# One-bank accumulator tiles for the later steps, and another order of the early steps, in a chunked linear-attention kernel with token routing

## The chip, the cores and the metric

The program runs on one core of one Trainium2 chip. A core has a matrix engine (TensorE, PE in the rows, with its weight loads as PEld), two engines that work along partitions and can read the accumulator memory PSUM (VectorE, DVE, and ScalarE, ACT), GpSimd (POOL), which cannot, and SyncE (SP), which here only issues transfers. Each engine runs its own stream in order, and semaphores order the streams against each other. The metric is the device time of one execution in microseconds (us); lower is better.

## The reference

For 4 batches, 8 heads, 768 positions and head size 64, the first half is decayed linear attention in blocks of 64. `lam` is one decay per head:

```
intra = (q_b k_b^T * Dmask) v_b              # Dmask[i,j] = lam^(i-j), i >= j
inter = (q_b * lam^(pos+1)) kv_state
out_b = intra + inter
kv_state = lam^64 * kv_state + (k_b * lam^(63-pos))^T v_b
```

The heads are then joined to rows x of 512. The second half routes tokens: scores = x . w_gate for each of the 768 positions of a batch, the 128 positions with the highest scores are taken, and for these out = x + sigmoid(score) * (relu(x w1) w2), with w1 of 512x1024 and w2 of 1024x512. All other rows stay x.

## The kernel before

**Steps.** The work is cut into 24 steps g of 128 positions, 6 for each batch. Steps 0 to 9 are "wide" (`wide(g)`, line 66): the 128 positions are one block of the attention, with masks and powers made for 128 (lines 135 to 158). Steps 10 to 23 are "narrow": two blocks of 64. Meanwhile w1 and w2 are loaded, and in narrow steps the expert products of an earlier batch are put in as "pieces" (`expert`, `products`), three to a step.

**A step's parts.** `transposes` makes q^T and k^T in PSUM with TensorE, `moved` copies them to SBUF with ScalarE (qT, kT). `queries_decayed` (POOL) makes qs from qT, `keys_decayed` (POOL) kd. `scores` multiplies kT and qT into the PSUM tile `su`; `masked` (DVE) takes it times the mask to p. `state_products` multiplies kd and v into `uu` (wide) or `su` (narrow), and `next_state` (DVE) adds the decayed old state. `from_scores` and `from_states` add up the output in the tile `o`; `outputs` (ScalarE) copies it out, `store` sends it to memory, `gate_scores` (DVE) takes the routing score. For the ranking, `row` transposes a column of scores, `compare` (DVE) makes a table of who beats whom, `column_sums` adds its columns up, and at the end of a batch `find`, `take` and `fetch` turn ranks into a list of tokens and gather their rows.

**PSUM.** It has 8 banks of 512 floats per partition. Four tiles of two banks each fill it: `su`, `o`, `uu`, `tt` (lines 181 to 184). In wide steps `tt` holds the transposes: q^T and k^T use the same columns, one after the other. In narrow steps the four banks of `uu` and `tt` are dealt out in turn by `bank()` (line 188) to transposes, rows, column sums and pieces, as slices of the two tiles:

```
free = [tt[:, 0], tt[:, 1]]
...
free[:0] = [uu[:, 0], uu[:, 1]]
```

**What sets the order.** The program order is written out by hand (`wide_step`, and the loop at the end). Each engine's stream follows it. The semaphores are put in by the framework: an instruction waits for those before it, on other engines, that touch the same tile.

Of the kernel before, what the change touches and what calls it, by code (L numbers as in the profile page):

```python
# [17 lines left out]
def kernel(  # L18
# [146 lines left out]
    def narrow_constants(g):  # L165
        if g == 0:
            for c in range(2):
                nc.scalar.copy(out=ident_c[half[c]], in_=ident[half[c], half[c]])
        elif g <= NHP:
            hp = g - 1  # L170
            for hh in range(2):
                h = 2 * hp + hh
                nc.vector.tensor_tensor_scan(
                    out=mask[:, hh, hp, :], data0=lam_b[:, h : h + 1].broadcast_to([128, C]),
                    data1=ident_c[:], initial=0.0, op0=ALU.mult, op1=ALU.add,
                )
        elif g == NHP + 1:
            nc.scalar.copy(out=kpow[:].rearrange("p a b -> p b a"), in_=mask[:, :, :, C - 1])
            nc.scalar.copy(out=decay[:], in_=qpow[:, :, C - 1 : C].broadcast_to([128, NHP, D]))
# [40 lines left out]
    pending = {}  # L220

    def transposes(g, name):
        if g >= NG:
            return
        t = loaded[g][1 if name == "qT" else 0]
        if not wide(g):
            tp = bank()
            pending[g, name] = tp[:]
            for hp in range(NHP):
                nc.tensor.transpose(  # L230
                    tp[:, hp * L : (hp + 1) * L], in_=t[:, 2 * hp : 2 * hp + 2, :],
                    identity=ident[:],
                )
            return
        tp = tt[:, :, : 2 * L]
        pending[g, name] = tp
        if name == "qT":
            to = tp.rearrange("p u (a i r) -> p u a r i", a=2, r=2)
        else:
            to = tp.rearrange("p u (a r i) -> p u a r i", a=2, r=2)  # L240
        for a in range(2):
            for r in range(2):
                for u, w in FOUR:
                    nc.tensor.matmul(  # L244
                        to[half[w], u, a, r], lhsT=t[half[u], 4 * a + 2 * w + r, :],
                        rhs=ident[half[u], half[u]], start=True, stop=True,
                        skip_group_check=True,
                    )

    def moved(g, name):  # L250
        if g >= NG:
            return
        dst = att.tile([128, NHP, L], FP32, name=name)
        src = pending.pop((g, name))
        if wide(g):
            nc.scalar.copy(out=dst[:].rearrange("p (u a) i -> p u (a i)", u=2), in_=src)  # L256
        else:
            nc.scalar.copy(out=dst[:].rearrange("p a i -> p (a i)"), in_=src)  # L258
        (qTs if name == "qT" else kTs)[g] = dst
# [15 lines left out]
    def scores(g, part=(0, 1)):  # L275
        if g >= NG:
            return
        if wide(g):
            qT, kT = qTs[g], kTs[g]
            if 1 in part:  # L280
                del qTs[g], kTs[g]
            for a in part:
# [10 lines left out]
        qT, kT = qTs.pop(g), kTs.pop(g)  # L293
# [140 lines left out]
    def settle(g):  # L434
        seen = mod.tile([128, 2], FP32, name="seen")
        if g % NT:
# [42 lines left out]
    def row(g):  # L479
# [8 lines left out]
        pb = uu[:, 0, 2 * D : 2 * D + L] if wide(g + 1) else bank()[:, :L]  # L488
# [3 lines left out]
        nc.scalar.copy(out=rows_[b][:, t * L : (t + 1) * L], in_=pb)  # L492
        fresh[g] = pb

# [25 lines left out]
    def column_sums(g):  # L520
# [4 lines left out]
        col = uu[:, 1, 2 * D : 2 * D + t] if wide(g + 2) else bank()[:, :t]  # L525
# [25 lines left out]
    def tokens(b, i):  # L551
        e = hits_.pop((b, i))
        pk = uu[:, 1, 3 * D : 3 * D + 2] if len(free) == 2 else bank()[:, :2]
# [171 lines left out]
    def wide_step(g):  # L725
        n = g + 1
        if g >= 0:
            if NGR:
                row(g - 1)
                column_sums(g - 2)  # L730
                compare(g - 1)
            queries_decayed(n)
# [7 lines left out]
        keys_decayed(n + 1)  # L740
        if wide(n):
            scores(n, (0,))
            from_states_wide(n, 1)
            scores(n, (1,))
        else:
# [9 lines left out]
        if NGR:  # L755
            if ends(g - 3):
                take((g - 3) // NT)
            if ends(g - 2):
                find((g - 2) // NT)

    for g in range(-1, NG):
# [3 lines left out]
        if g < 0:  # L765
            transposes(0, "qT")
            moved(0, "qT")
            transposes(0, "kT")
            moved(0, "kT")
# [3 lines left out]
        if wide(g):  # L773
            wide_step(g)
            if g >= 0:
                narrow_constants(g)
# [87 lines left out]
```

## Time and profile before

| what | value |
|---|---|
| median of 3 runs | 228.57 us (227.01 to 232.99) |
| the profiled execution | 227.02 us, of which the span of the instructions is 225.2 us |
| TensorE busy, instructions | 172.0 us (76%), 4412 matmuls and 4412 weight loads |
| VectorE, ScalarE, GpSimd busy | 109.0, 68.3, 89.2 us |
| mean granted TensorE clock | 0.977 of 2.4 GHz |
| memory traffic | 32.36 MB in all, 144 GB/s |

Busy time of TensorE is that of pipelined instructions, and no measure of its peak. What counts for a change of order is which wait ends last in a stretch; the rows below show for each stretch what TensorE does and what ended its idle time. A matmul of the program in float32 is two matmuls and two weight loads in the profile (the transposes of 128x128 are one of each), so "x16" in the order is "x32" in a row.

### The profile page before, as it was taken

Reading aid. Unit: us, or ns where it says so; the run is one execution under the profiler, and the core shown is the slowest. Engines: PE = TensorE matmul, PEld = TensorE weight load, DVE = VectorE, ACT = ScalarE, POOL = GpSimd, SP = SyncE. Lnnn points to the kernel's source line nnn. Section 1 sums busy time; section 2 is a strip of 40 time slices with the busy share of each in tenths; the row PEclk is TensorE's granted clock in tenths of the full one; section 3 lists DMA queues with packets and bytes.
Section 4 is the critical chain, followed back from the end, with each engine's and each line's share of the span. In section 5 each row is a group of like instructions: output and inputs, shape, how many; then the busy total and the mean of one; then the engine's idle time right before and its main releaser. Section 6 shows DMA issues by size and latency. Waiting matters only on the chain.

```text
span 225.2 us, 9940 instructions
## 1 busy us (share of the span) xinstructions
PE 172.0 (76%) x4412; PEld 135.2 (60%) x4412; DVE 109.0 (48%) x358; ACT 68.3 (30%) x169; POOL 89.2 (40%) x101
## 2 busy tenths in 40 slices
PE   0875686665876876887998878899889677888990
PEld 0865585554765764775854648788446567646940
DVE  4651666773436462634566364655655535352001
ACT  2233322332222233434422444355224332302300
POOL 3563544425245267065348344554466410012001
PEclk9999979999698899999999999999999999999999
DMA  4766665689697594187467989945013101102001
GB/s 114 201 182 190 195 204 174 198 245 257 174 232 180 159 264 163 56 225 182 156 139 184 261 196 233 245 118 133 1 49 97 68 31 47 49 5 88 3 0 47
DMA packets 67626, 32.36 MB, mean 144 GB/s; under 512 B 45440, under 2 KB 62848, under 8 KB 67584
## 3 DMA queue, kind: packets, MB, share of 16 engines
q1 hardware_dynamic: 66800, 29.63, 48.6%
q0 software_dynamic: 640, 2.10, 2.6%
q8 instruction: 35, 0.57, 1.0%
q14 instruction: 7, 0.06, 0.1%
q10 hardware_dynamic: 144, 0.00, 0.0%
HBM read 24.38 MB, written 7.34 MB: 141 GB/s over the span
## 4 chain that ended last, share of the span: by engine, by line
PE 63%; issue 14%; ACT 10%; POOL 4%; DVE 4%; DMA 3%; SPq 1%; POOLq 1%; ACTq 0%; DVEq 0%
PE tt L633 7%; PE uu L621 7%; PE tt L244 6%; PE o L418 5%; PE tt L621 4%; PE su L286 4%; PE o L427 4%; PE o L402 4%; PE tt L230 3%; PE su L339 3%; PE uu L633 3%; PE uu L230 3%; PE su L295 3%; ACT qT L256 2%; PE o L387 2%
## 5 line engine op out<-in xcount | busy, mean ns | idle before, releaser
L268 POOL TENSOR_TENSOR qs<-qT,qpow 128x512 f32<-128x512 f32 x14 | 17.8, 1272 | 37.2 <-ACT qT L258 36.9
L621 PE MATMUL uu<-xsT,w_sb 128*128 128x128 f32 x152 | 21.4, 284 | 3.7 <-ACT kT L258 1.2
L621 PEld LDWEIGHTS uu<-xsT,w_sb 128*128 128x128 f32 x152 | 18.5, 192 | 5.4 <-ACT hs L625 1.7
L352 POOL TENSOR_TENSOR decayed<-state,decay 128x256 f32<-128x256 f32 x23 | 17.5, 761 | 9.0 <-DVE state L377 8.8
L633 PE MATMUL tt<-w_sb,hs 128*128 128x512 f32 x32 | 17.3, 632 | 1.8 <-DVE beat L501 0.9
L469 DVE CUSTOM_DVE_ANT_0 xg<-x_b,wg_b 128x512 f32<-128x512 f32 x24 | 16.5, 688 | 1.9 <-ACT x_b L457 1.2
L312 DVE TENSOR_TENSOR p<-su,mask 128x512 f32<-128x512 f32 x14 | 9.7, 692 | 14.8 <-PE su L295 14.8
L352 POOL TENSOR_TENSOR decayed<-state,decay_w 128x256 f32<-128x256 f32 x7 | 7.4, 1052 | 23.7 <-DVE state L377 17.6
L266 POOL TENSOR_TENSOR qs<-qT,qpow 128x512 f32<-128x512 f32 x9 | 11.5, 1275 | 11.7 <-ACT qT L256 11.7
L418 PE MATMUL o<-vn,p 64*64 64x64 f32 x640 | 14.8, 246 | 0.6 <-issue 0.6
L621 PE MATMUL tt<-xsT,w_sb 128*128 128x128 f32 x104 | 14.1, 279 | 1.1 <-ACT qT L258 0.7
L633 PE MATMUL uu<-w_sb,hs 128*128 128x512 f32 x32 | 14.6, 598 | 0.3 <-DVE ranks L531 0.3
L418 PEld LDWEIGHTS o<-vn,p 64*64 64x64 f32 x640 | 12.9, 157 | 3.1 <-issue 1.9
L214 POOL TENSOR_TENSOR kd<-kn,kpow 128x512 f32<-128x512 f32 x14 | 14.6, 1042 | 0.0
L244 PE MATMUL tt<-ident,qn 64*64 64x64 f32 x320 | 8.5, 229 | 8.0 <-DMA qn<-in_q_dram 5.3
L256 ACT COPY qT<-tt 128x512 f32<-128x512 f32 x10 | 5.9, 586 | 28.1 <-PE tt L244 25.9
L305 DVE TENSOR_TENSOR p<-su,mask_w 128x1024 f32<-128x1024 f32 x10 | 12.2, 1224 | 4.4 <-PE su L286 3.9
L244 PE MATMUL tt<-ident,kn 64*64 64x64 f32 x320 | 8.0, 242 | 8.3 <-ACT qT L256 7.3
L286 PE MATMUL su<-qT,kT 64*64 64x128 f32 x320 | 14.3, 288 | 0.0
L621 PEld LDWEIGHTS tt<-xsT,w_sb 128*128 128x128 f32 x104 | 12.7, 192 | 1.7 <-ACT qT L258 0.9
L650 POOL DMA_INDIRECT out_dram<-y,tok x4 | 4.2, 1054 | 23.8 <-DVE y L646 23.8
L579 POOL DMA_INDIRECT xs<-out_dram,tok x4 | 4.2, 1040 | 21.9 <-DVE tok L562 21.9
(111 smaller groups left out, 355.1 us busy)
## 6 DMA issues: line engine op xcount, KB each, us to landing
out_dram<-x_b SPq DMA_DIRECT2D x24, 256.0 KB, 2.6
w_sb<-in_moe_w_dram SPq DMA_DIRECT2D x8, 512.0 KB, 5.4
kn<-in_k_dram SPq DMA_DIRECT2D x14, 256.0 KB, 3.9
qn<-in_q_dram SPq DMA_DIRECT2D x14, 256.0 KB, 4.8
vn<-in_v_dram SPq DMA_DIRECT2D x14, 256.0 KB, 5.0
kn<-in_k_dram SPq DMA_DIRECT2D x20, 128.0 KB, 3.7
qn<-in_q_dram SPq DMA_DIRECT2D x20, 128.0 KB, 3.1
vn<-in_v_dram SPq DMA_DIRECT2D x20, 128.0 KB, 3.7
```

The source lines that it names most:

```text
L214: nc.gpsimd.tensor_tensor(out=kd[:], in0=loaded[g][0][:], in1=pw.unsqueeze(2).broadcast_to([128, H, D]), op=ALU.mult,)
L230: nc.tensor.transpose(tp[:, hp * L : (hp + 1) * L], in_=t[:, 2 * hp : 2 * hp + 2, :], identity=ident[:],)
L244: nc.tensor.matmul(to[half[w], u, a, r], lhsT=t[half[u], 4 * a + 2 * w + r, :], rhs=ident[half[u], half[u]], start=True, stop=True, skip_g ...
L266: nc.gpsimd.tensor_tensor(out=qs[:], in0=qTs[g][:], in1=qpow[:], op=ALU.mult)
L268: nc.gpsimd.tensor_tensor(out=qs[:].rearrange("p a (c i) -> p a c i", c=2), in0=qTs[g][:].rearrange("p a (c i) -> p a c i", c=2), in1=qpow ...
L286: nc.tensor.matmul(su[half[u], w, m * L : (m + 1) * L], lhsT=kT[half[w], 2 * u + a, r * C : (r + 1) * C], rhs=qT[half[w], 2 * u + a, :], s ...
L305: nc.vector.tensor_tensor(out=p[:], in0=su[:], in1=mask_w[:].rearrange("p w a r i -> p w (a r i)"), op=ALU.mult,)
L352: nc.gpsimd.tensor_tensor(out=t[:], in0=states[n][:], in1=(decay_w if wide(g) else decay)[:], op=ALU.mult)
L418: nc.tensor.matmul(o_[half[m], u, (2 * a + w) * D : (2 * a + w + 1) * D], lhsT=p[half[u], w, i0 : i0 + C], rhs=vn[half[u], 4 * a + 2 * w + ...
L469: nc.vector.tensor_tensor_reduce(out=xg[:], in0=x_bs[b][:, t].rearrange("p a b e -> p (a b e)"), in1=wg_b[:], scale=1.0, scalar=0.0, op0=A ...
L621: nc.tensor.matmul(ph, lhsT=w1_sb[:, dc, f * 128 : (f + 1) * 128], rhs=keep["xsT"][:, dc, :], start=(dc == 0), stop=(dc == NDC - 1),)
L633: nc.tensor.matmul(py[:], lhsT=keep["hs"][:, f, :], rhs=w2_sb[:, f, :], start=(f == 0), stop=(f == NFC - 1),)
```

## The change

Four things are changed.

1. **PSUM tiles.** `uu` and `tt` come from a pool of their own (`pair`), which is closed when the wide steps end; `single_banks` then opens a pool of four tiles m0 to m3 of one bank each, and `bank()` deals these out.
2. **Transposes of wide steps.** q^T and k^T lie in different columns of `tt`, and the two copies by ScalarE come after both.
3. **Order of a wide step.** Scores and mask of step n = g + 1 come first, then the transposes of n + 1, then the outputs of g, the state products of n, and only then `row`, `column_sums` and the second half of `from_states` (`from_states_wide(n, 1)`). Before, scores were split in two around that half, rows and column sums came first and transposes last. The copy of the score row moves behind the column sums (`row_copied`), and `compare` reads the copy instead of PSUM. A small copy by ScalarE out of `o` (`settle`) follows the second half.
4. **Constants of narrow steps.** The eight scans for the narrow mask on DVE, and the two copies for them on ScalarE, move from the ends of wide steps 0 to 4 to the very start.

```diff
-    uu = psum.tile([128, 2, 512], FP32, name="uu")
-    tt = psum.tile([128, 2, 512], FP32, name="tt")
-    free = [tt[:, 0], tt[:, 1]]
-    held = []
+    early = ExitStack()
+    pair = early.enter_context(tc.tile_pool(name="pair", bufs=1, space=PSUM))
+    uu = pair.tile([128, 2, 512], FP32, name="uu")
+    tt = pair.tile([128, 2, 512], FP32, name="tt")
+    free, held = [], []
+
+    def single_banks():
+        early.close()
+        late = ctx.enter_context(tc.tile_pool(name="late", bufs=1, space=PSUM))
+        free.extend(late.tile([128, 512], FP32, name=f"m{i}") for i in range(4))
...
+    def row_copied(g):
+        if not 0 <= g < NG:
+            return
+        b, t = divmod(g, NT)
+        nc.scalar.copy(out=rows_[b][:, t * L : (t + 1) * L], in_=fresh[g])
+        if not free:
+            fresh[g] = rows_[b][:, t * L : (t + 1) * L]
...
     def wide_step(g):
         n = g + 1
+        scores(n)
+        masked(n)
+        if wide(n):
+            transposes(n + 1)
+            queries_decayed(n + 1)
         if g >= 0:
-            if NGR:
-                row(g - 1)
-                column_sums(g - 2)
-                compare(g - 1)
-            queries_decayed(n)
             from_scores(g)
             from_states_wide(g, 0)
             outputs(g)
...
         keys_decayed(n + 1)
+        second(n)
+        if g >= 0 and NGR:
+            row(g - 1)
+            column_sums(g - 2)
+            if ends(g - 3):
+                take((g - 3) // NT)
+            row_copied(g - 1)
+            compare(g - 1)
         if wide(n):
-            scores(n, (0,))
             from_states_wide(n, 1)
-            scores(n, (1,))
-        else:
-            scores(n)
+            settle(n)
         if g >= 0:
             gate_scores(g)
-        masked(n)
-        second(n)
-        if wide(n):
-            for name in ("qT", "kT"):
-                transposes(n + 1, name)
-                moved(n + 1, name)
...
             if not wide(g + 1):
-                free[:0] = [uu[:, 0], uu[:, 1]]
+                single_banks()
```

**Place 1: TensorE in an early step (g = 1, which puts out step 1 and prepares steps 2 and 3).** Before; L489 is the score row, L418 and L387 the outputs from scores and from states, L329 the state products, L286 the scores, L244 the transposes:

```order
L489 MATMUL uu<-ident,sc 128x128
L418 MATMUL o<-vn,p 64x64 x32
L387 MATMUL o<-state,qs 64x64 x8
L329 MATMUL uu<-vn,kd 64x64 x16
L286 MATMUL su<-qT,kT 64x128 x8
L387 MATMUL o<-state,qs 64x64 x8
L286 MATMUL su<-qT,kT 64x128 x8
L244 MATMUL tt<-ident,qn 64x64 x16
L244 MATMUL tt<-ident,kn 64x64 x16
```

and with the change, in its own line numbers (L289 scores, L249 transposes, L420 and L389 outputs, L331 state products, L495 row):

```order
L289 MATMUL su<-qT,kT 64x128 x16
L249 MATMUL tt<-ident,qn 64x64 x16
L249 MATMUL tt<-ident,kn 64x64 x16
L420 MATMUL o<-vn,p 64x64 x32
L389 MATMUL o<-state,qs 64x64 x8
L331 MATMUL uu<-vn,kd 64x64 x16
L495 MATMUL uu<-ident,sc 128x128
L389 MATMUL o<-state,qs 64x64 x8
```

The same matmuls stand in both; the row now stands directly behind the state products, which write the same tile, and the outputs from scores stand between the transposes and whatever needs their copies.

**Place 2: TensorE in the first narrow steps, with the semaphores that each row waits for.** Before (L230 the narrow transposes, L402 the outputs from states, L592 the transposes of gathered rows, L527 column sums):

```order
L230 MATMUL uu<-ident,qn 128x128 [waits DMAHW3_49]
L230 MATMUL uu<-ident,qn 128x128 x3
L230 MATMUL uu<-ident,kn 128x128 [waits DMAHW2_49,Activation_49]
L230 MATMUL uu<-ident,kn 128x128 x3
...
L592 MATMUL tt<-ident,xs 128x128 [waits DMASW0_49]
L592 MATMUL tt<-ident,xs 128x128 x3
L527 LDWEIGHTS table
L527 MATMUL tt<-ones,table 128x1 [waits Activation_49]
```

and with the change:

```order
L233 MATMUL m_1718<-ident,qn 128x128 [waits DMAHW3_49,Activation_49]
L233 MATMUL m_1718<-ident,qn 128x128 x3
L233 MATMUL m_1719<-ident,kn 128x128 [waits DMAHW2_49]
L233 MATMUL m_1719<-ident,kn 128x128 x3
...
L607 MATMUL m_1720<-ident,xs 128x128 [waits DMASW0_49]
L607 MATMUL m_1720<-ident,xs 128x128 x3
L542 LDWEIGHTS table [waits DVE_49]
L542 MATMUL m_1721<-ones,table 128x1
```

The transposes of k, and the column sums, no longer wait for ScalarE; they write a tile of their own, where before they wrote the second bank of a tile whose first bank was being copied out.

**Place 3: DVE at the start.** Before:

```order
L151 SCALAR_TENSOR_TENSOR qpow<-lam_p,zero 128x128 x4
L372 COPY state<-uu 128x256
L305 TENSOR_TENSOR p<-su,mask_w 128x1024
L377 TENSOR_TENSOR state<-uu,decayed 128x256
```

and with the change:

```order
L151 SCALAR_TENSOR_TENSOR qpow<-lam_p,zero 128x128 x4
L170 SCALAR_TENSOR_TENSOR mask<-lam_b,ident_c 128x64 x8
L307 TENSOR_TENSOR p<-su,mask_w 128x1024
L374 COPY state<-uu 128x256
L307 TENSOR_TENSOR p<-su,mask_w 128x1024
```

Eight scans now stand ahead of the first mask.

## Rows read from the trace of the kernel before

**Rows 1.** The page's chain that ended last: share of the span by engine.
```profile
PE 63%; issue 14%; ACT 10%; POOL 4%; DVE 4%; DMA 3%; SPq 1%; POOLq 1%; ACTq 0%; DVEq 0%
```

**Rows 2.** Stretches: us; busy us (x) of PE, PEld, DVE, ACT, POOL; clock, DMA, GB/s.
```profile
5.00:84.00 79.00, 56.22 (x2243) 49.29 (x2247) 43.98 (x122) 21.35 (x45) 35.16 (x38) 0.94 0.74 203
84.00:200.00 116.00, 96.33 (x2086) 73.35 (x2077) 60.50 (x223) 42.74 (x113) 49.08 (x52) 1.00 0.48 130
```

**Rows 3.** Timeline, TensorE, early steps: start, length, instructions [idle before, releaser].
```profile
18.89 0.69 PE L244 MATMUL tt<-ident,kn 64*64 64x64 f32 x32 [0.68 <-ACT qT L256]
...
22.03 0.34 PE L387 MATMUL o<-state,qs 64*64 64x64 f32 x5 [0.88 <-issue]
...
26.67 0.57 PE L244 MATMUL tt<-ident,kn 64*64 64x64 f32 x23 [1.02 <-issue]
...
48.37 0.21 PE L527 MATMUL uu<-ones,table 128*128 128x1 bf16 x3 [0.67 <-ACT sc_row L492]
```

**Rows 4.** Sums by stretch between "issue" stalls of TensorE; columns as in Rows 2.
```profile
9.30:75.88 66.58, 46.91 (x1920) 41.31 (x1915) 34.59 (x96) 17.70 (x39) 28.33 (x29) 0.92 0.74 203
22.03:26.67 4.64, 2.86 (x127) 2.57 (x127) 3.60 (x6) 1.17 (x2) 3.19 (x3) 1.00 0.64 191
26.67:30.38 3.71, 3.71 (x128) 3.43 (x127) 1.07 (x6) 1.24 (x3) 0.14 (x1) 0.61 0.77 231
```

**Rows 5.** DMA queues, stretch 24.30 to 25.35: packets, MB, share of engines.
```profile
q8 instruction: 1, 0.02, 5.6%
```

**Rows 6.** TensorE's groups, 84 to 200: busy us, mean ns | idle before, releasers.
```profile
L633 PE MATMUL tt<-w_sb,hs 128*128 128x512 f32 x32 | 17.3, 632 | 1.8 <-DVE beat L501 0.9 <-ACT sc_row L492 0.7
L621 PE MATMUL uu<-xsT,w_sb 128*128 128x128 f32 x120 | 17.0, 285 | 3.0 <-ACT kT L258 1.2 <-ACT hs L625 1.1 <-ACT sc_row L492 0.7
L621 PE MATMUL tt<-xsT,w_sb 128*128 128x128 f32 x72 | 9.9, 281 | 1.1 <-ACT qT L258 0.7 <-ACT sc_row L492 0.4
...
L402 PE MATMUL o<-state,qs 64*64 64x64 f32 x416 | 9.7, 224 | 1.2 <-ACT x_b L457 0.9 <-POOL decayed L352 0.3
L339 PE MATMUL su<-vn,kd 64*64 64x64 f32 x368 | 9.1, 219 | 0.4 <-issue 0.4
...
L230 PE MATMUL uu<-ident,kn 128*128 128x128 f32 x32 | 5.0, 278 | 2.3 <-ACT qT L258 2.3
...
L230 PE MATMUL tt<-ident,qn 128*128 128x128 f32 x24 | 3.9, 286 | 2.2 <-DVE y L646 2.2
L230 PE MATMUL tt<-ident,kn 128*128 128x128 f32 x20 | 3.1, 278 | 2.4 <-DVE y L646 1.6 <-ACT qT L258 0.8
...
L489 PE MATMUL uu<-ident,sc 128*128 128x128 f32 x8 | 2.5, 313 | 1.6 <-ACT xsT L597 0.6 <-DVE ranks L531 0.6 <-ACT hs L625 0.3
L489 PE MATMUL tt<-ident,sc 128*128 128x128 f32 x7 | 2.2, 314 | 1.3 <-ACT hs L625 0.7 <-DVE ranks L531 0.7
L527 PE MATMUL tt<-ones,table 128*128 128x1 bf16 x21 | 1.7, 165 | 1.0 <-ACT xsT L597 0.7 <-ACT hs L625 0.4
L527 PE MATMUL uu<-ones,table 128*128 128x1 bf16 x23 | 1.4, 164 | 1.1 <-DVE table L510 0.7 <-ACT hs L625 0.4
```

**Rows 7.** Timeline, TensorE: transposes of k in two narrow steps.
```profile
102.88 0.66 PE L230 MATMUL tt<-ident,kn 128*128 128x128 f32 x4 [0.81 <-ACT qT L258]
...
117.80 0.60 PE L230 MATMUL uu<-ident,kn 128*128 128x128 f32 x4
```

**Rows 8.** Timeline, TensorE: scores right behind state products of the same tile.
```profile
83.57 0.69 PE L295 MATMUL su<-qT,kT 64*64 64x64 f32 x32 [0.69 <-DVE state L377]
```

**Rows 9.** Timeline, DVE: scans, and the first mask.
```profile
6.88 2.18 DVE L151 TENSOR_TENSOR_SCAN qpow<-lam_p,zero 128x128 f32<-128x128 f32 x4
...
11.09 1.23 DVE L305 TENSOR_TENSOR p<-su,mask_w 128x1024 f32<-128x1024 f32 x1 [0.97 <-PE su L286]
...
25.24 1.71 DVE L173 TENSOR_TENSOR_SCAN mask<-lam_b,ident_c 128x64 f32<-128x64 f32 x2
...
33.27 0.68 DVE L173 TENSOR_TENSOR_SCAN mask<-lam_b,ident_c 128x64 f32<-128x64 f32 x2
```

More of the change, by code (lines that the diff above doesn't have):

```diff
@@ L218, in keys_decayed, with transposes @@
         kds[g] = kd
-    pending = {}
-    def transposes(g, name):
+    def transposes(g):
         if g >= NG:
             return
[L225 to L238, printed above, removed]
-        else:
[L240 to L247, printed above, removed]
-                    )
@@ L250, in moved @@
-    def moved(g, name):
-        if g >= NG:
-            return
+        from_ = {"qT": loaded[g][1], "kT": loaded[g][0]}
+        tp = {}
+        for name, t in from_.items():
+            if not wide(g):
+                tp[name] = bank() if free else tt[:, len(tp)]
+                for hp in range(NHP):
+                    nc.tensor.transpose(
+                        tp[name][:, hp * L : (hp + 1) * L], in_=t[:, 2 * hp : 2 * hp + 2, :],
+                        identity=ident[:],
+                    )
+                if free:
+                    moved(g, name, tp[name][:])
+                continue
+            if name == "qT":
+                tp[name] = tt[:, :, : 2 * L]
+                to = tp[name].rearrange("p u (a i r) -> p u a r i", a=2, r=2)
+            else:
+                tp[name] = tt[:, :, 2 * L :]
+                to = tp[name].rearrange("p u (a r i) -> p u a r i", a=2, r=2)
+            for a in range(2):
+                for r in range(2):
+                    for u, w in FOUR:
+                        nc.tensor.matmul(
+                            to[half[w], u, a, r], lhsT=t[half[u], 4 * a + 2 * w + r, :],
+                            rhs=ident[half[u], half[u]], start=True, stop=True,
+                            skip_group_check=True,
+                        )
@@ L273, in queries_decayed, with scores @@
         qss[g] = qs
-    def scores(g, part=(0, 1)):
+    def scores(g):
         if g >= NG:
             return
+        qT, kT = qTs.pop(g), kTs.pop(g)
         if wide(g):
[L279 to L282, printed above, removed]
+            for a in range(2):
                 for r in range(2):
@@ L435, in settle @@
         seen = mod.tile([128, 2], FP32, name="seen")
+        if wide(g):
+            if g % NT:
+                nc.scalar.copy(out=seen[:], in_=o_[:, :, 0])
+            return
         if g % NT:
@@ L487, in row @@
             ranks[b] = mod.tile([128, NT], FP32, name="ranks")
-        pb = uu[:, 0, 2 * D : 2 * D + L] if wide(g + 1) else bank()[:, :L]
+        pb = uu[:, 0, 2 * D : 2 * D + L] if not free else bank()[:, :L]
         nc.tensor.transpose(
@@ L491, in row @@
         )
-        nc.scalar.copy(out=rows_[b][:, t * L : (t + 1) * L], in_=pb)
         fresh[g] = pb
+        if free:
+            row_copied(g)
+    def row_copied(g):
+        if not 0 <= g < NG:
+            return
+        b, t = divmod(g, NT)
+        nc.scalar.copy(out=rows_[b][:, t * L : (t + 1) * L], in_=fresh[g])
+        if not free:
+            fresh[g] = rows_[b][:, t * L : (t + 1) * L]
     def compare(g):
@@ L524, in column_sums @@
         table = tables.pop(g)
-        col = uu[:, 1, 2 * D : 2 * D + t] if wide(g + 2) else bank()[:, :t]
+        col = uu[:, 1, 2 * D : 2 * D + t] if not free else bank()[:, :t]
         for j in range(t):
@@ L552, in tokens @@
         e = hits_.pop((b, i))
-        pk = uu[:, 1, 3 * D : 3 * D + 2] if len(free) == 2 else bank()[:, :2]
+        pk = uu[:, 1, 3 * D : 3 * D + 2] if not free else bank()[:, :2]
         for t in range(NT):
```

59 lines of the change are left out of this document (24 added, 35 removed).

## The prediction

> **What bounds the kernel now.** I read four views in this order: the chain that ended last, the sums by stretch, TensorE's timeline, and its groups with what ended their idle time. The chain [rows 1] is mostly TensorE, then "issue", time in which the engine waited for nothing that the profile shows. So TensorE's stream is to be read, and it has two parts [rows 2]: the early (wide) steps until about 84 us, where TensorE is busy for 56.2 of 79.0 us, and the late (narrow) steps until 200, busy for 96.3 of 116.0 us, idle for 19.7. The clock is at 0.94 of 2.4 GHz in the first and full in the second.
>
> In the **early part** three kinds of idle time repeat [rows 3]: the transposes of k wait 0.68 us for the copy of qT, the column sums wait 0.67 us for the copy of the score row, and now and then TensorE stops for about 1 us on "issue". The last kind is the key. From one such stop to the next (second and third row of [rows 4]) lie 127 or 128 matmuls and 127 weight loads each, together 256 instructions with the one or two that a count of starts misses. Between them one packet of 0.02 MB passes on the queue named "instruction" [rows 5]; it is moving at about 24.3 to 25.3, 2.3 us after TensorE went on at 22.03, and TensorE goes on again at 26.67, 1.4 us after it [rows 3]. So TensorE's instructions come in blocks of 256, the next block is fetched only when the one before it has been begun, and fetch and start together take some 4 us, while the 256 instructions themselves need 2.9 us at full clock [rows 4]. Over the long stretch (first row of [rows 4]) 1920 + 1915 = 3835 instructions, 15.0 blocks, take 66.6 us: 4.44 us a block, which is the price of a fetch and not of the work. A wait of 0.7 us inside a block shortens the stop at its end by as much. The early part is bound by the supply of TensorE's instructions.
>
> In the **late part** a matmul of 128x128 takes 0.28 us and the instructions are fewer in a us (4163 in 116.0 us, 7.1 us a block), so the blocks mostly come in time: "issue" ended 0.4 us of idle time at a matmul [rows 6]. Here the idle time has other names, and they fit one reading: a matmul that writes one bank of a tile waits for an engine that reads the tile's other bank. The pair in [rows 7] shows it: k's transposes wait 0.81 us for the copy of qT where both lie in `tt`, and not at all where q went to the other tile. With the change these waits are gone from the list of semaphores (second place in the order above).
>
> **The change part by part.**
>
> *One-bank tiles.* From [rows 6] I sum what a tile of its own takes away: L633 1.8, L621 3.0 and 1.1, L230 2.3, 2.2 and 2.4, L489 1.6 and 1.3, L527 1.0 and, of 1.1, the 0.4 on ScalarE: **17.1 us**. What stays is true need: 0.9 on the copy out of `o`, 0.7 on the table, 0.3 on POOL, 0.4 on issue. TensorE is the engine that the others wait for in this stretch (DVE is busy for 60.5 of 116 us, ScalarE 42.7, POOL 49.1), so idle time taken from it is time taken from the end.
>
> *What is late next there.* With 17.1 us less, a block of 256 lasts 116.0 - 17.1 = 98.9 us over 16.3 blocks, 6.1 us on the mean; the mean stays above a fetch, but a block made only of short matmuls doesn't. Below, this costs nothing; above, 4.4 us (a fetch as in the early part) less the 2.9 us that 256 short matmuls take, on perhaps a quarter of 16 blocks: 4 x 1.5 = 6 us. I take **2 us**, nearer the low end, because only one such stop of 0.4 us is to be seen now. The copy of x_b, too, was covered by the wait for qT that goes; the 0.9 us in [rows 6] is the price where it is not covered, and between the two stand a step's scores and transposes, so I put it at nothing, and at up to 4 us for the range.
>
> *Order of the early steps.* The waits for qT (0.68 us, once a step) and for the score row (0.67 us, in the six or so steps that have column sums) go [rows 3]. A new one comes: the row stands directly behind the state products and writes the same tile, so it waits until DVE has read the state; the nearest row is 0.69 us [rows 8], nine times, and the second half of the outputs is queued behind it. Neither the gain of about 11 us nor the loss of about 6 us reaches the end while a block's fetch takes 4.44 us and a block holds 2.9 us of work: I take **0**, and keep -11 and +6 as ends. The loads are asked for in the same order behind the same stores, the copies by ScalarE are two small ones more in a stretch where it is busy for 21 of 79 us, and POOL's work is unchanged. The skill speaks against this order: by the Trainium skill, PSUM — Partial Sum Buffer, section "PSUM bank collisions raise a hardware error", an engine's accesses are to be kept apart by bank and not by address, so the row cannot slip past DVE's read although its columns are others. By that rule alone the early part would lose the six us; by the fetch it loses nothing.
>
> *The seam.* Between 75.9 and 84 us one wait of 0.69 us [rows 8], one for qT and some short ones go, partly under a fetch: **-1 us**.
>
> *Scans to the start.* DVE is free of its first scans at 6.88 + 2.18 = 9.06 us [rows 9] and did the first mask at 11.09. Now eight scans stand ahead of it: 0.34 us each where DVE ran alone (0.68 for two), 0.85 where POOL worked beside it (1.71 for two). The mask then starts between 11.8 and 15.9 us, 0.7 to 4.8 us later; but only the scores of the next step need its end, and ahead of these TensorE has that step's transposes and the first state products to do, and a fetch to wait for. I take **+0.5 us**, ends -0.5 and +3. Later, the two scans a step that DVE no longer does stood in its idle time: nothing.
>
> **Sum**, against the profiled execution: 227.0 - 17.1 + 2 + 0 - 1 + 0.5 = 211.4, say **212 us**. That execution lies 1.6 us below the median of the runs shown (228.57) and at the fastest of them, so I read 212 as a run of the ordinary kind.
>
> **Rivals.**
>
> *Half comes back* (0.20). The late steps get shorter, blocks of short matmuls arrive late, x_b is uncovered, or DVE, which has 60 us of work in 99, becomes late for the scores. With the upper ends of both, 6 + 4 in place of 2: 227.0 - 17.1 + 10 - 0.5 = 219. For it: every block in the early part shows what a fetch costs. Against: most late blocks have 2 us to spare.
>
> *The early steps gain too* (0.12). If a block can come earlier than I read it, 11 us more go: 201. The Trainium skill, Runtime: NRT & Kernel Launch, section "Terms", calls the instruction memory a FIFO of 32 to 128 KiB that is refilled in blocks of 16 KiB; with several blocks ahead no fetch would be seen, and this rival would hold. The trace has blocks of that size and TensorE waiting for each, so I give it little.
>
> *The change does not do what it says* (0.06). If the late waits are only where TensorE happens to wait for a chain on POOL or DVE that goes on being the same length, or the loads set the pace, the time stays within 2%, about 226. Against: the waits go from engine to engine with the tile and not with the work.
>
> *Slower* (0.03). The new waits of the early steps make them a serial chain at the lower clock. At 0.61 of the clock 256 instructions took 3.71 us instead of 2.86 [rows 4]; at 1.2 GHz throughout I estimate 4.5, a step of 1.75 blocks 7.9 us, and if the waits for the state (0.69), for x_b (0.9) and for the copy of kT (0.7, as that of qT now) all stood bare, 10.2 us a step against 7.8 now (1.75 x 4.44). Ten steps: +24, in all 227.0 + 24 - 15.6 = 235. It decides as soon as a step's waits end later than its next block; the granted clock would have to stay near 1.2 GHz from 5 to 84 us, and it is at 0.94 now.
>
> **How the numbers follow.** The forecast has 0.59. Its own bounds (start, fetch, x_b) reach from 208 to 217; with "half comes back" and the nearer part of the early gain, 204 to 221 leaves out 0.2. A measurement of this kernel can tell about 2% from no change, that is a time below 224 or above 233. Faster: forecast, half and early gain, 0.59 + 0.20 + 0.12 less a little for their edges, 0.90. Within 2%: 0.07. Slower: 0.03.
>
> **What would show it.** In the changed profile: k's transposes and the pieces of late steps without waits for ScalarE or DVE; TensorE idle below 6 us of a late part of about 100 us; in the early part still 256 instructions from stop to stop at about 4.4 us, the waits for qT gone and the stops on "issue" longer by as much; a wait for the state of about 0.7 us ahead of the row. I am wrong if blocks follow each other in 3 us, or if the late part stays near 116 us.

## The result, and the profile after

The changed kernel took **214.19 us** (median of five runs, 207.04 to 217.54); the kernel before took 228.81 in the same series. The ratio is **0.911, interval 0.900 to 0.922**. This ratio, and those in the table of runs, set the fast runs of both kernels against each other (for the changed kernel 207.04 and 209.01 us, at a granted clock of 0.96; the others, at 0.83 to 0.93, took 211.4 to 217.5), so 0.911 is not the quotient of the two medians, which is 0.936. Forecast: 212, range 204 to 221.

The trace taken with the result is that of its longest run (217.54 us, granted clock 0.81 and 0.84 of 2.4 GHz in the two stretches), so I read a second trace of the same kernel beside it (run a_again below, 207.64 us; some of the expectations call it the second look). Stretches as in [rows 2], first the trace of the result, then the second trace:

```profile
5.00:84.00 79.00, 60.07 (x2246) 55.45 (x2247) 41.18 (x115) 21.48 (x50) 32.55 (x37) 0.81 0.70 194
84.00:200.00 116.00, 110.49 (x2132) 86.52 (x2132) 63.60 (x234) 43.93 (x120) 51.40 (x54) 0.84 0.52 140
```

```profile
5.00:84.00 79.00, 55.27 (x2247) 50.18 (x2247) 41.77 (x116) 21.50 (x50) 32.82 (x38) 0.94 0.72 199
84.00:200.00 116.00, 110.75 (x2164) 86.26 (x2165) 64.69 (x235) 44.80 (x124) 51.21 (x54) 0.99 0.50 137
```

Until 84 us TensorE has done as many instructions as before (2247 against 2243), at either clock; behind it, it is idle for 5 us in place of 20. For an exact cut I take the first transposes of q in step 10, which end the early part in both orders: at 84.20 us before, at 85.35 now. From there to the end, before and in the second trace:

```profile
84.20:225.20 141.00, 115.53 (x2171) 85.76 (x2165) 63.12 (x229) 45.63 (x123) 52.04 (x55) 1.00 0.41 112
```

```profile
85.35:205.90 120.55, 111.44 (x2165) 86.26 (x2165) 64.94 (x234) 44.53 (x123) 50.84 (x54) 0.98 0.48 131
```

The early part, with a new wait of 1.97 us at its end, lost 1.2 us, and the late part gained 20.4: 16.4 of idle time (25.5 to 9.1) and 4.1 of TensorE's busy time, though the number of its instructions is the same. TensorE's groups in 84 to 200 us of the second trace, which answer to [rows 6]:

```profile
L636 PE MATMUL m<-xsT,w_sb 128*128 128x128 f32 x256 | 32.2, 280 | 2.1 <-ACT xsT L612 1.6 <-issue 0.5
L648 PE MATMUL m<-w_sb,hs 128*128 128x512 f32 x63 | 30.5, 605 | 0.0
L404 PE MATMUL o<-state,qs 64*64 64x64 f32 x416 | 10.1, 231 | 0.9 <-ACT x_b L463 0.9
...
L233 PE MATMUL m<-ident,qn 128*128 128x128 f32 x52 | 8.5, 286 | 2.0 <-ACT sc_row L506 2.0
L233 PE MATMUL m<-ident,kn 128*128 128x128 f32 x52 | 8.3, 284 | 0.0
...
L495 PE MATMUL m<-ident,sc 128*128 128x128 f32 x15 | 4.5, 300 | 0.0
L542 PE MATMUL m<-ones,table 128*128 128x1 bf16 x44 | 3.1, 165 | 0.8 <-DVE table L525 0.8
```

Every wait that [rows 6] puts down to the other half of a tile is gone; what is left are true needs (xsT, x_b, table) and one wait of 2.0 us at the seam. L648 shows where busy time went as well. Two of its steps before, then one now:

```profile
114.40 1.88 PE L633 MATMUL tt<-w_sb,hs 128*128 128x512 f32 x4
...
121.19 1.12 PE L633 MATMUL tt<-w_sb,hs 128*128 128x512 f32 x2 [0.35 <-ACT sc_row L492]
122.77 1.13 PE L633 MATMUL tt<-w_sb,hs 128*128 128x512 f32 x2 [0.45 <-DVE beat L501]
```

```profile
115.77 1.88 PE L648 MATMUL m<-w_sb,hs 128*128 128x512 f32 x4
```

Four matmuls in a row take 1.88 us; cut by a wait they take 1.12 + 1.13 and the wait of 0.45 besides. So a stop here costs its idle time and, on top, the overlap of the matmuls that it cuts apart.

Early, the waits changed places. Waits of TensorE in 5 to 84 us, as sum, times and longest, before and in the second trace:

```profile
PE tt L244 <- ACT qT L256: 7.3, 10, 0.8
...
PE uu L527 <- ACT sc_row L492: 4.2, 6, 1.2
PE tt L244 <- issue: 3.6, 3, 1.6
PE o L387 <- issue: 2.4, 3, 1.1
PE uu L329 <- issue: 2.1, 1, 2.1
```

```profile
PE o L420 <- issue: 8.3, 5, 2.8
...
PE uu L495 <- DVE state L379: 3.9, 6, 0.9
PE uu L331 <- issue: 3.3, 2, 2.1
PE o L389 <- issue: 1.9, 1, 1.9
PE su L289 <- issue: 1.6, 2, 0.8
PE su L289 <- ACT kT L263: 1.5, 2, 1.2
PE tt L249 <- issue: 1.1, 1, 1.1
```

The waits for qT and the score row gave back 11.5 us. In their place came 13.4: 7.5 more on "issue" (from 8.7, with a group of 0.6 not shown, to 16.2), 4.4 for the state (with one of 0.5 not shown) and 1.5 for kT. Blocks of 256 instructions follow each other as before: 2050 + 2045 = 4095 instructions, 16.0 blocks, in 70.8 us are 4.43 us a block, against 4.44 in [rows 4].

A block's end looks as before, too. In 23.60 to 25.15 one packet passes, as in [rows 5]; TensorE has run dry in the state products and goes on at 26.29, 1.1 us after that stretch, and the row behind them waits for the state:

```profile
q8 instruction: 1, 0.02, 5.7%
```

```profile
26.29 0.33 PE L331 MATMUL uu<-vn,kd 64*64 64x64 f32 x3 [2.08 <-issue]
27.20 0.32 PE L495 MATMUL uu<-ident,sc 128*128 128x128 f32 x1 [0.59 <-DVE state L379]
```

The 16 blocks of the second trace, in one stretch:

```profile
10.26:81.06 70.80, 49.05 (x2050) 44.54 (x2045) 34.97 (x96) 19.84 (x47) 29.69 (x32) 0.93 0.71 197
```

In that stretch the queue "instruction" has 16 packets of 0.02 MB, one a block; each starts 0.4 to 2.9 us after its block has begun and takes 0.9 to 1.6 us, and 13 of the 16 next blocks begin 1.2 to 1.6 us after its end. Over the whole run the page counts 34 such packets, and 4412 matmuls and 4412 weight loads are 34.5 blocks of 256.

### The profile page after: what moved, and what is told of

The parts are those of the page before. It is cut to its first block, busy times and chain, and to the rows that moved or that the text cites. A ratio compares the mean times of both kernels' runs of the same rounds, so it can differ in the third digit from the quotient of the medians.

```text
span 215.8 us, 9910 instructions
## 1 busy us (share of the span) xinstructions
PE 181.2 (84%) x4412; PEld 147.4 (68%) x4412; DVE 107.6 (50%) x358; ACT 68.1 (32%) x177; POOL 86.7 (40%) x101
## 4 chain that ended last, share of the span: by engine, by line
PE 72%; issue 15%; ACT 3%; DMA 3%; DVE 2%; POOL 2%; SPq 1%; POOLq 1%; DVEq 0%; ACTq 0%
PE m L636 12%; PE m L648 11%; PE m L233 7%; PE tt L249 7%; PE su L289 6%; PE o L420 5%; PE o L404 4%; PE o L429 4%; PE su L341 3%; PE su L297 3%; PE o L389 3%; PE uu L331 2%; DMA out_dram<-y,tok 1%; DMA qn<-in_q_dram 1%; DVE state L379 1%
## 5 line engine op out<-in xcount | busy, mean ns | idle before, releaser
L636 PE MATMUL m<-xsT,w_sb 128*128 128x128 f32 x256 | 35.4, 297 | 2.1 <-ACT xsT L612 2.1
L636 PEld LDWEIGHTS m<-xsT,w_sb 128*128 128x128 f32 x256 | 33.1, 209 | 3.3 <-ACT xsT L612 3.0
L648 PE MATMUL m<-w_sb,hs 128*128 128x512 f32 x64 | 35.2, 680 | 0.0
L420 PE MATMUL o<-vn,p 64*64 64x64 f32 x640 | 15.4, 242 | 6.6 <-issue 6.6
L420 PEld LDWEIGHTS o<-vn,p 64*64 64x64 f32 x640 | 13.8, 157 | 7.5 <-issue 7.5
L648 PEld LDWEIGHTS m<-w_sb,hs 128*128 128x128 f32 x64 | 11.5, 200 | 9.9 <-issue 9.5
L289 PE MATMUL su<-qT,kT 64*64 64x128 f32 x320 | 15.7, 349 | 1.5 <-ACT kT L263 1.5
L640 ACT ACTIVATE hs<-m 128x128 f32<-128x128 f32 x32 | 8.9, 277 | 25.4 <-PE m L636 24.2
L249 PE MATMUL tt<-ident,qn 64*64 64x64 f32 x320 | 10.3, 275 | 6.0 <-DMA qn<-in_q_dram 5.2
L249 PEld LDWEIGHTS tt<-ident,qn 64*64 64x64 f32 x320 | 9.8, 184 | 6.4 <-issue 6.1
L289 PEld LDWEIGHTS su<-qT,kT 64*64 64x64 f32 x320 | 12.7, 175 | 2.1 <-ACT kT L263 1.9
L379 DVE TENSOR_TENSOR state<-su,decayed 128x256 f32<-128x256 f32 x23 | 9.7, 424 | 8.2 <-PE su L341 5.1
L429 PEld LDWEIGHTS o<-vn,p 64*64 64x64 f32 x448 | 8.1, 138 | 6.4 <-DVE table L525 1.8
```

The costliest lines, as they stand in the source:

```text
L249: nc.tensor.matmul(to[half[w], u, a, r], lhsT=t[half[u], 4 * a + 2 * w + r, :], rhs=ident[half[u], half[u]], start=True, stop=True, skip_g ...
L289: nc.tensor.matmul(su[half[u], w, m * L : (m + 1) * L], lhsT=kT[half[w], 2 * u + a, r * C : (r + 1) * C], rhs=qT[half[w], 2 * u + a, :], s ...
L420: nc.tensor.matmul(o_[half[m], u, (2 * a + w) * D : (2 * a + w + 1) * D], lhsT=p[half[u], w, i0 : i0 + C], rhs=vn[half[u], 4 * a + 2 * w + ...
L429: nc.tensor.matmul(o_[half[hh ^ c], hh, hp * D : (hp + 1) * D], lhsT=p[half[c], hh, hp * C : (hp + 1) * C], rhs=vn[half[c], 2 * hp + hh, : ...
L636: nc.tensor.matmul(ph, lhsT=w1_sb[:, dc, f * 128 : (f + 1) * 128], rhs=keep["xsT"][:, dc, :], start=(dc == 0), stop=(dc == NDC - 1),)
L648: nc.tensor.matmul(py[:], lhsT=keep["hs"][:, f, :], rhs=w2_sb[:, f, :], start=(f == 0), stop=(f == NFC - 1),)
```

## The experiments

Theory: the early part is bound by the supply of TensorE's instructions, the late part was bound by waits between the two banks of one tile. Rivals: the early order gains too; the late waits come from something else. All times in us. "Step 10" is when the first transposes of q of step 10 begin in the trace, "then" what is left to the end of the span; "before" is the median of the kernel before in the same series; a ratio to it stands with its interval, where there is one.

| run | median (range) | before | ratio | step 10 | then |
|---|---|---|---|---|---|
| kernel before | | | | 84.20 | 141.0 |
| a_again | 210.57 (207.64 to 212.58) | 231.56 | 0.915 (0.899 to 0.930) | 85.35 | 120.6 |
| tiles_alone | 210.81 (207.57 to 211.86) | 231.56 | 0.907 (0.892 to 0.922) | 89.71 | 120.1 |
| order_alone | 230.32 (226.28 to 231.18) | 231.56 | | 86.80 | 141.7 |
| few_transposes | 205.49 (204.11 to 208.66) | 231.56 | 0.891 (0.881 to 0.900) | 83.77 | 123.1 |
| wait_again | 211.03 (210.26 to 211.82) | 230.98 | 0.920 (0.914 to 0.926) | 88.68 | 121.3 |
| more_matmuls | 217.10 (216.46 to 217.92) | 230.98 | 0.947 (0.940 to 0.953) | 93.78 | 122.3 |
| alternate | 234.00 (232.27 to 237.96) | 230.98 | 1.017 (1.008 to 1.027) | 86.41 | 145.2 |
| first_quads | 202.05 (200.66 to 204.35) | 230.98 | 0.879 (0.869 to 0.888) | 81.60 | 121.0 |
| apart | 225.98 (223.27 to 227.69) | 230.69 | 0.981 (0.950 to 1.011) | 84.31 | 141.2 |
| few_old_order | 205.73 (204.44 to 207.88) | 230.69 | 0.896 (0.871 to 0.922) | 83.98 | 120.7 |
| row_first | 202.07 (199.60 to 204.48) | 230.69 | 0.885 (0.854 to 0.916) | 76.78 | 121.0 |
| scans_late | 210.68 (207.04 to 212.50) | 230.69 | | 84.24 | 122.1 |

### Which half holds the gain

**a_again**, the changed kernel.

> The changed kernel once more, unchanged, for a second trace of it. Theory (the prediction's): the late part holds the gain, the early part none, so at a granted clock like that of the kernel before (0.97) the trace shows TensorE's last wide-step instruction as late as before within 2 us, blocks of 256 instructions still about 4.4 us apart, and 207 to 213 us in all. Rival (the early order gains too): the early part ends 4 to 11 us earlier than before, and the time at a full clock lies below 207 us.

Met: blocks at 4.43 us, step 10 at 85.35.

**tiles_alone**, the kernel before with

```
+ early = ExitStack(); pair = early.enter_context(tc.tile_pool(...))   # uu, tt
+ early.close()     # ahead of step 10; then four tiles [128, 512] from a new pool
- free[:0] = [uu[:, 0], uu[:, 1]]
```

> The kernel before with nothing but the new pools: uu and tt in a pool that is closed after the last wide step, and four one-bank tiles from then on; the early order as before. Theory: the waits between the two halves of one tile were the late part's loss, so nearly all of the gain is here: ratio to before 0.91 to 0.94 (208 to 215 us). Rival (early order gains too): 0.95 to 0.97 (217 to 222 us), the rest coming from the order.

**order_alone**, the changed kernel with `single_banks()` giving out `uu[:, 0], uu[:, 1], tt[:, 0], tt[:, 1]`.

> The changed kernel with its early order, its joint copies and its scans at the start, but the late steps again deal out the four banks of the two two-bank tiles. Theory: the early part is bound by the supply of TensorE's instructions, whose number is the same, so ratio 0.985 to 1.005 (225 to 230 us). Rival (early order gains too): 0.95 to 0.975 (217 to 223 us).

Both as the theory has them, and they add up: the tiles alone 0.907, the order alone 230.32 against 231.56. The last column says it: in the traces of the kernel before and of these three runs it is 120 or 121 us with one-bank tiles, 141 or 142 without, whatever the early order.

The column "step 10" must be read with its spread. It lies between 84.20 and 89.71 in the four traces with the old early order (kernel before, tiles_alone, alternate, apart) and between 84.24 and 86.80 in the four with the new one (the trace of the result with 86.14, a_again, order_alone, scans_late). A difference of 1 to 3 us between two single traces shows nothing there; the 1.2 us that the early part lost is one of these.

### What bounds the early part

**wait_again**, the changed kernel with

```
- tp[name] = tt[:, :, 2 * L :]      # kT
+ tp[name] = tt[:, :, : 2 * L]      # the columns of qT
+ moved(g, name, tp[name])          # and each copied at once
```

> The changed kernel, but in the wide steps the k transposes again write the columns of the q transposes, so that they wait for the copy of qT, and the copies go one by one. Theory (supply of instructions bounds the early part): the ten waits of some 0.7 us that come back stand where TensorE would wait for its next block anyway: 0 to 2 us more than the changed kernel in the same traces' early part (its seam at 87 us against 87), in all 207 to 211 us. Rival (the chain between the engines bounds): ten times 0.7 us come back: 213 to 217 us.

The ten waits came back, and the blocks hardly felt them:

```profile
PE tt L249 <- ACT qT L264: 7.4, 10, 0.8
```

```profile
10.97:83.69 72.72, 52.76 (x2046) 47.73 (x2041) 35.34 (x88) 20.77 (x47) 29.16 (x31) 0.86 0.66 183
```

16.0 blocks in 72.7 us, 1.9 us more for 7.4 us of waits. Step 10 came 3.3 us later than in the second trace (88.68 against 85.35), more than the theory's 2, but at a lower granted clock as well (0.86 against 0.93 in the 16 blocks). The time, 211.03, is at the upper end of what the theory gives, and 2 us below the rival's lowest.

**more_matmuls**, the changed kernel with, in each wide step,

```
+ for _ in range(4):
+     for u, w in FOUR:
+         nc.tensor.matmul(uu[half[w], u, 4 * D : 5 * D], lhsT=loaded[n][2][half[u], w, :],
+                          rhs=ident[half[u], half[u]], ...)
```

> The changed kernel with 16 matmuls of 64x64 more in each of the ten wide steps, on loaded values into columns of uu that nothing reads: 64 instructions a step, 640 in all, and no other engine has more to do. Theory (supply of instructions): 640 instructions are 2.5 blocks at 4.4 us, 11 us more: 218 to 222 us at the clock of the second look. Rival 1 (work): 16 such matmuls take 0.35 us, so 3.5 us more: 211 to 213 us. Rival 2 (the chain between the engines bounds, TensorE has slack): 0 to 1 us more: 207 to 210 us.

217.1: below the theory's 218, and 4 us above what the work allows. By the medians the 640 instructions cost 6.5 us (217.10 against 210.57 in another series), 2.6 us for each of the 2.5 blocks; by step 10 of the two traces 8.4 us, 3.4 a block. Both lie between 4.4 (supply alone) and 1.4 (work alone). The blocks came a little faster than in the second trace, 4.28 us each (2179 + 2177 instructions are 17.0 blocks), though the clock was lower and TensorE had more to do:

```profile
10.31:83.06 72.75, 54.06 (x2179) 49.64 (x2177) 29.20 (x86) 17.85 (x43) 26.22 (x28) 0.86 0.65 182
```

**few_transposes**, the changed kernel with

```
- for u, w in FOUR:   # 64 rows each
-     nc.tensor.matmul(to[half[w], u, a, r], lhsT=t[half[u], 4 * a + 2 * w + r, :],
-                      rhs=ident[half[u], half[u]], ...)
+ for w in range(2):  # 128 rows each, into one bank a tensor
+     nc.tensor.matmul(to[half[w], :, a, r], lhsT=t[:, 4 * a + 2 * w + r, :], rhs=ident[:], ...)
```

> The changed kernel with the transposes of a wide step written as 8 matmuls of 128 rows and 64 stationary columns a tensor in place of 16 of 64x64, into one bank a tensor: the same products, half the instructions, 64 fewer a step, 640 in all. Theory (supply of instructions): 640 instructions are 2.5 blocks of 256 at 4.44 us, so the early part ends 8 to 11 us earlier: 8 to 11 us less than the changed kernel in the same runs. Rival (TensorE's work or the chain between engines bounds): the work of these transposes goes from 19.6 us to some 16 (the wide scores' 49 ns a matmul, twice that where only two fit side by side), so 0 to 4 us less.

5.1 us less by the medians, between both. Two things in the trace can have taken the rest; first_quads below gives the first of them back, no run measures the second, and the traced run is the longest of this series (208.66 us). The first transposes of 128 rows need both halves of a loaded tile, and the first scores began 1.9 us later, at 10.65 against 8.71 in the second trace (timeline of this run):

```profile
5.81 1.98 PE L248 MATMUL tt<-ident,qn 128*64 128x128 f32 x16 [5.81 <-DMA qn<-in_q_dram]
...
10.65 1.99 PE L285 MATMUL su<-qT,kT 64*64 64x128 f32 x32 [1.16 <-ACT kT L259]
```

And a block held more work: 47.64 us busy over 13.0 blocks are 3.7 us, where the second trace has 49.05 over 16.0, 3.1; a wait inside a block is then less often covered, as I read it. The blocks came 4.67 us apart:

```profile
19.82:80.50 60.68, 47.64 (x1667) 41.81 (x1660) 33.53 (x92) 18.36 (x45) 27.45 (x29) 0.97 0.75 207
```

**few_old_order**, few transposes in the early order of the kernel before, with one-bank tiles late.

> The early order of the kernel before (scores split around the state products, row ahead of the outputs, k transposes into the columns of the q transposes) with the few transposes of the step before last and one-bank tiles late: what the new early order is worth once TensorE needs one block less in each 4. Theory: supply still bounds, 384 instructions a step are 1.5 blocks, so the order is worth little: 0 to 3 us more than the kernel with few transposes and the new order (202.1): 202 to 205 us. Rival (with fewer instructions the chain between the engines bounds, so the waits of the old order come back): 5 to 10 us more: 207 to 212 us.

205.73 where first_quads has 202.05 (another series): 3.7 us, just above the theory's 3 and below the rival's 5. With fewer instructions the new order seems to begin to be worth something; I can't say more, since row_first, in the same series, differs by 3.7 as well but also has another seam.

**scans_late**, the eight scans back at the ends of the wide steps.

> The changed kernel with the eight scans of the narrow mask back at the ends of the wide steps, two a step. Prediction's term: the scans at the start cost 0.5 us (between 0.5 gained and 3 lost), so 0 to 0.5 us less than the changed kernel, with the first wide scores at 8.7 us of the trace as before and the second at 13.6. Rival (at the start they delay the masks of step 0): 2 to 3 us less. Rival (late they stand ahead of the state sums on DVE): 1 to 2 us more.

210.68 where the changed kernel has 210.57 and 214.19 in its two series: no difference to be seen, in times that lie up to 5 us apart within a series. Against the rival of the delayed masks speaks the trace: the first two masks start at 11.00 and 15.01 us here, and at 10.76 and 15.04 in the second trace. The rival of 1 to 2 us more is not excluded.

### What the late waits are

**alternate**, the kernel before with

```
- free[:0] = [uu[:, 0], uu[:, 1]]
+ free[:] = [uu[:, 0], tt[:, 0], uu[:, 1], tt[:, 1]]
```

> The kernel before, with its two-bank tiles to the end, but the late steps take the four banks in the order uu 0, tt 0, uu 1, tt 1 in place of uu 0, uu 1, tt 0, tt 1. Theory (a write to one bank of a two-bank tile waits for the readers of the other): the write now comes two grants later instead of one, when the reader of the other bank is mostly done, so 8 to 17 us of the late waits go: ratio 0.925 to 0.965. Rival (the waits come from too few banks, or from pools): 0.99 to 1.01.

Missed: 1.7% slower. The experiment did not do what I meant it to. Banks are held for the expert's sums, which shifts the turn, so that neighbours still come from one tile. Its trace tells the tiles apart all the same (timeline, k's transposes with q's ahead of them):

```profile
101.92 0.66 PE L230 MATMUL uu<-ident,qn 128*128 128x128 f32 x4
102.41 0.60 PE L230 MATMUL tt<-ident,kn 128*128 128x128 f32 x4
...
116.39 0.66 PE L230 MATMUL uu<-ident,qn 128*128 128x128 f32 x4
117.86 0.66 PE L230 MATMUL uu<-ident,kn 128*128 128x128 f32 x4 [0.81 <-ACT qT L258]
```

In the kernel before, in alternate and in order_alone there are 39 such pairs. k waits for the copy of qT in all 12 in which both drew the same tile and in none of the 27 others.

**apart**, the kernel before with a rule for neighbours:

```
- t = next(t for t in free if not any(t is x for x in held))
+ can = [x for x in free if not any(x is y for y in held)]
+ apart = [x for x in can if len(free) == 4 and of[id(x)] != last[0]]     # of the other tile
+ t = (apart or can)[0]
+ last[0] = of.get(id(t))     # the tile of the bank given out
```

> The kernel before, with its two-bank tiles to the end, but each grant of a bank in the late part takes a bank of the other tile than the grant before it (where one is not held). The order uu, tt, uu, tt alone did not do that: a held bank shifts the turn, and the k transposes there waited for the copy of qT exactly in the 4 of 13 steps in which both drew the same tile. Theory (a write to one bank of a tile waits for the readers of the tile's other bank): with no two grants in a row from one tile most of the late waits go, 8 to 14 us: 217 to 223 us where the kernel before shows 231, and no k transpose waits for qT. Rival (the waits come from the number of banks, or move to the grant after): 228 to 233 us.

Nearer to the rival than to the theory: 4.7 us less by the medians, and the interval takes in no change. In its trace the late part is as long as before, but at a lower granted clock (0.94 against 1.00): TensorE is busy for 5.1 us more and idle for 4.9 us less (20.6 in place of 25.5):

```profile
84.31:225.50 141.19, 120.63 (x2171) 91.10 (x2165) 62.36 (x229) 45.16 (x123) 51.95 (x55) 0.94 0.41 109
```

No k transpose waits for qT directly any more, but other waits of the same kind stayed. Its timeline, TensorE, then ScalarE and VectorE:

```profile
109.59 0.30 PE L493 MATMUL tt<-ident,sc 128*128 128x128 f32 x1
110.25 1.12 PE L637 MATMUL tt<-w_sb,hs 128*128 128x512 f32 x2 [0.35 <-ACT sc_row L496]
111.83 1.13 PE L637 MATMUL tt<-w_sb,hs 128*128 128x512 f32 x2 [0.45 <-DVE beat L505]
```

```profile
109.93 0.27 ACT L496 COPY sc_row<-tt 128x128 f32<-128x128 f32 x1 [2.24 <-PE tt L493]
```

```profile
111.42 0.35 DVE L505 SCALAR_TENSOR_TENSOR beat<-tt,sc,lead 128x128 bf16<-128x128 f32 x1 [1.02 <-PE tt L637]
```

The expert's sum holds one bank of `tt`; the score row went to the other. The sum goes on only when the row has been copied (110.25), and again when DVE has compared it (111.83), though neither touches the held bank. No order of grants avoids that while one bank is held for several pieces: either its mate is given out, or neighbours come from the other tile. A tile of its own does (L648 in the second trace, no idle time). So the reading of the waits stands on tiles_alone and on the 39 pairs; my size for this run was wrong.

### A faster kernel

**first_quads**, few_transposes with step 0 in 64x64 pieces as in the changed kernel, and the new tiles dealt out from the banks of `tt` on (`m[i] for i in (2, 3, 0, 1)`).

> The run with few transposes, with two changes: step 0 keeps its 64x64 transposes, which need only one half of a loaded tile each, and the new one-bank tiles are dealt out beginning with the banks of tt, whose readers are done by then, in place of those of uu. Theory: with few transposes the first scores began 1.9 us later than in the second look at the changed kernel (10.65 against 8.71), which comes back in part (1 to 3 us), and the wait of 1.97 us at the seam goes (1 to 2 us): 200 to 203 us. Rival (the first block fetch, not the loads, delays the start, and the wait at the seam only moves to the next step): 204 to 206 us.

202.05, 3.4 us less than few_transposes by the medians (of two series): the start came back (first scores at 8.94). The second half fell: the wait at the seam is still 1.97 us.

```profile
81.60 0.66 PE L234 MATMUL m<-ident,qn 128*128 128x128 f32 x4 [1.97 <-ACT sc_row L521]
```

So the first write to the new pool waits for the last reader of the old one, whichever bank comes first. What made that reader late is in the second trace (ScalarE, then VectorE):

```profile
85.03 0.27 ACT L506 COPY sc_row<-uu 128x128 f32<-128x128 f32 x1 [1.75 <-DVE ranks L546]
```

```profile
84.51 0.42 DVE L379 TENSOR_TENSOR state<-su,decayed 128x256 f32<-128x256 f32 x1 [0.84 <-POOL decayed L354]
84.85 0.14 DVE L546 TENSOR_TENSOR ranks<-ranks,uu 128x1 f32<-128x1 f32 x1
```

**row_first**, first_quads with, in the last wide step, `row`, `column_sums` and `row_copied` ahead of `state_products`.

> The kernel with few transposes, with row, column sums and the row's copy of the last wide step ahead of that step's state products. At the seam the first write to the new one-bank tiles waited 1.97 us for the copy of sc_row, whichever bank came first, so the release of the old tiles waits for their last reader; that copy waited for DVE's ranks, and these for a state sum that waited for GpSimd. Theory: the copy is done 1.5 us earlier and the wait at the seam falls to under 0.7 us: 200 to 201.5 us. Rival (the state sum is late next, and the seam waits for it elsewhere): 202 us.

The wait at the seam is gone from the trace, and 0.8 us came back as a wait of the state products for kd. Step 10 began at 76.78 in place of 81.60, more than the 2 us of the seam; the rest lies in the blocks ahead of it, which I did not take apart. The trace of first_quads is also of its longest run (204.35 us), and this one of its shortest (199.60).

```profile
76.78 0.66 PE L234 MATMUL m<-ident,qn 128*128 128x128 f32 x4
...
79.26 0.68 PE L356 MATMUL su<-vn,kd 64*64 64x64 f32 x16 [0.77 <-POOL kd L219]
```

Its median of 202.07 is that of first_quads in another series, its fastest run 199.60 against 200.66; the seam's 2 us are too little for these intervals. Both beat the kernel before by some 12% (0.879 and 0.885), and the changed kernel's 210.57 by some 8.5 us.

## Why the prediction was right

**One-bank tiles, 17.1 us.** Right in kind, too small: the late part gave 20.4. The waits that I summed went, and with them 16.4 us of idle time behind step 10. On top came 4.1 us of busy time, since a stop also breaks the overlap of matmuls (1.12 + 1.13 against 1.88); the granted clock was no higher (0.98 against 1.00). I had priced stops by their idle time alone.

**New stops, +2 us.** Wrong in size: one "issue" stop of 0.5 us late, as there was one of 0.4 before, and x_b at 0.9 as before. Late blocks got shorter and stayed long enough.

**Early order, 0.** Right, and in the main for the reason given. 11.5 us of waits went and the blocks still came 4.43 us apart; "issue" stops took up most, the waits for the state and for kT the rest. order_alone and wait_again show both directions, at the clocks that they had. The new waits ahead of the row are there, 0.5 to 0.9 us, 4.4 us in seven where I had counted nine and 6 us. By the Trainium skill, PSUM — Partial Sum Buffer, section "PSUM bank collisions raise a hardware error", columns in one bank don't set two engines apart; these waits fit that, but no run here shows it, since the semaphores go by tile and hold an engine off the other bank of a tile as well. With those waits alone the early part would have lost 4.4 us; it lost 1.2, less than the 1.97 at its seam.

**The seam, -1 us.** Wrong: it cost about 2 us (1.97 on the copy of the last score row), also in order_alone. I looked at which waits go at 84 us, and not at who reads the old tiles last in the new order.

**Scans at the start, +0.5 us.** Not distinguishable from nothing. The eight took 1.69 us, less than the 2.7 to 6.8 that I allowed, and the first mask came earlier than in [rows 9] (timeline of the second trace):

```profile
8.98 1.69 DVE L170 TENSOR_TENSOR_SCAN mask<-lam_b,ident_c 128x64 f32<-128x64 f32 x8
10.76 1.22 DVE L307 TENSOR_TENSOR p<-su,mask_w 128x1024 f32<-128x1024 f32 x1
```

**The sum.** In the second trace the late part is 5.3 us better than forecast (20.4 gained against 17.1 - 2), and the early part with the seam 1.7 us worse (1.2 lost against 0.5 gained): 207.6 us where I had 211.4. The two errors cancel for a part only. That the median of the result's series lies as near to 212 as it does is luck: its runs go from 207.0 to 217.5 us, and the forecast was worked out from a run of the kernel before at a clock of 0.977, so the run that compares with it is that of 207.6 us at 0.966.

**Rivals.** "The early steps gain too" fell with order_alone. It rested on the size of the instruction memory in the Trainium skill, Runtime: NRT & Kernel Launch, section "Terms" (a FIFO of 32 to 128 KiB, refilled in blocks of 16 KiB), which I had taken for room for several blocks ahead. The second trace agrees with the size of a block (one packet of 0.02 MB for each) and not with my reading: the next block mostly begins 1.2 to 1.6 us behind its packet. more_matmuls limits my own reading: a block more cost 2.6 to 3.4 us and not 4.4, so supply bounds the early part in the main, and what a block holds (its work, and waits inside it such as the state's) for a part. How much each, and what sets the start of a fetch, stays open. "Half comes back" and "slower" fell with the late part at 120.6 us and the early part at 85. In "slower" I had also put the block at half clock too high: the two rows that it names (2.86 us at 1.00, 3.71 at 0.61), on a straight line in one over the clock, give 4.2 us and not 4.5, and a total near 230, hardly slower at all. "The change does not do what it says" fell with tiles_alone.

## What to carry to other kernels

Where a wait on TensorE changes its releaser with the bank and not with the work, look for a tile that spans several banks, and give each bank a tile of its own, above all one that is held long. Where "issue" stops come at even counts of instructions, moving waits is worth little and fewer instructions are worth more, but only as long as the work that each carries does not grow as much. Price a stop of TensorE by its idle time and by the overlap that it breaks: here 16.4 and 4.1 us.

## What I had not expected of the hardware

- With the new early order the pace did not follow the granted clock: 4.43 us a block at 0.93, 4.28 at 0.86 (more_matmuls), and until 84 us as many matmuls at 0.81 as at 0.94 (2246 and 2247). With the waits for qT it may: 4.55 at 0.86 (wait_again), and in the old order step 10 at 84.20 after a clock of 0.94 (kernel before) and at 89.71 after 0.86 (tiles_alone). So the order may be worth some us at a low clock; no run here was made to show it.
- The timeline shows 35 stops of TensorE behind the seam before and 6 now (without the wait at the seam itself), at an equal count of instructions; with the 29 went 4.1 us of busy time, 0.14 us each on the mean.
